# Attention and a gated feed-forward on one core: the engines' instructions in another order, found by a longer search

## The chip, the cores and the metric

The kernel runs on one core of a Trainium2 chip. The metric is the device time of one execution in microseconds, as the median of several runs.

## The reference

```python
q_d, k_d, v_d = mean over groups of 4 positions of q, k, v          # 576 -> 144
out_up = repeat(softmax(q_d k_d^T / 8) v_d, 4)
out_local = softmax(where(|i - j| < 4, q k^T / 8, -1e9)) v           # a band of 7
x = (out_up + out_local) as (batch * position, head * 64)            # 4608 x 512
out = ((x @ w1) * (x @ w2) @ w3) @ w_out
```

There are 8 batches of 8 heads, 576 positions and 64 dimensions; w1 and w2 are 512 x 1024, w3 is 1024 x 1024, w_out 1024 x 512. Activations are float32; the weights are given in 64 bits.

## The kernel before

**The fold.** Since nothing stands between w3 and w_out, their product is made once (`fold`, line 362 on): 64 products of 128 x 128 x 512, `accw`, each two matmul records. The 64-bit weights are loaded raw by SP (`words`, line 335) into a ring of six buffers `raw` and are turned to float32 by two passes on ScalarE (lines 342 and 350, the latter sometimes on VectorE, 354) and a join on VectorE (357). The gate weights w1 and w2 (`gate_weights`) come the same way, and are split into a high and a low part (436, 438).

**Attention.** For batches 0 to 2 it is done on TensorE: `pooled_sums` loads q and k in four phases (`q4` by line 635, `k4` by line 654), VectorE adds them up into `qks` (617) and reorders q into `qn` (641); `group_unit` makes the banded scores `se_ps` (723), `quad` the pooled scores `s_ps` (538), their maxima (543), exponentials (553), scaling (567 on ScalarE, 570 on GpSimd for later batches) and transposes `t_ps` (581), which ScalarE copies to `pt` (588, 590); `te_ps` and `pte` (693, 700) are the same of the banded scores. `group_values` and `pooled` multiply with v (`oe_ps` 772, `o_ps` 499). The pooled v is added up by GpSimd's accumulating DMAs (461). For batches 3 to 7 the banded part is done by VectorE and ScalarE (`unit`, line 857 on): products `pr` (884), their sums, a softmax, products `pv` with v, which are added up in `xl`, three of the six additions by an accumulating DMA that GpSimd issues (959).

**The feed-forward.** The 4608 tokens are nine chunks of 512. For each chunk and each f of 8, `moe` makes `pab` (two gates, 24 matmuls of 512 columns: three per product, with high and low parts), copies one on ScalarE (`a`, 1038), multiplies on VectorE (1040), splits into `gh` (ScalarE, 1044) and `gl` (VectorE, 1049), and multiplies with the folded weight into `acc` (`down`, 96 matmuls per f and four chunk rows of 128).

**What sets the order.** Every step is a task with an engine, a cost, what it needs and the buffers (`Ring`) it takes. The order on each engine is written out in `ORDER`, a table of task numbers by engine. `Plan.order` walks the five lists with the tasks' costs and merges them into one order of recording; it does not change the order within an engine. Semaphores then make each instruction wait for what it needs, and each engine takes its own list strictly in order.

```python
for e, l in mine.items():
    left[e] = [l[k] for w in ORDER[e].split() for a, _, b in [w.partition("-")] for k in range(int(a), int(b or a) + 1)][::-1]

def mm_us(n):
    return n * 0.418e-3 + 0.0135
```

Of the kernel before, what the change touches and what calls it, by code (L numbers as in the profile page):

```python
# [100 lines left out]
    ),  # L101
    DVE=(
# [164 lines left out]
def mm_us(n):  # L267
    return n * 0.418e-3 + 0.0135
# [973 lines left out]
```

## Time and profile before

| | |
|---|---|
| median of 3 runs | 778.26 us (775.34 to 779.37) |
| the profiled execution | 777.15 us, its span 775.0 us |
| TensorE busy | 748.4 us (97%), weight loads 574.7 us (74%) |
| VectorE busy | 575.0 us (74%) |
| ScalarE busy | 495.6 us (64%) |
| GpSimd busy | 136.0 us (18%) |
| HBM | 111 GB/s over the span |

The span runs from the first to the last instruction. The program has a first stage to about 104 us, in which the fold and the attention of the first tokens share TensorE while the queues load the weights; a middle in which the chunks' matmuls run while VectorE and ScalarE make the next tokens; and a last 120 us in which TensorE works alone. Busy times of TensorE overlap from one matmul to the next, and a matmul at half clock counts as busy.

### The profile page before, as it was taken

To read this page: it belongs to the slowest core of one execution; us is meant where nothing else is said; L and a number is where in the kernel's file an instruction comes from. 1 tells how busy PE (TensorE), PEld (TensorE's weight loads), DVE (VectorE), ACT (ScalarE), POOL (GpSimd) and SP (SyncE) were. 2 spreads that over 40 slices of the span, in tenths; PEclk is the share of its full clock that TensorE was granted. 3 is DMA by queue.
4 is the path that set the end of the run, shared out by engine and by line. 5 is a ranking of instruction groups with operands and counts; after the bars stand their busy time and mean duration, and the time that the engine had idled before them with its cause. 6 is when DMAs were issued, how large, how long until landed. Compare 5 with 4: busy or idle time off the path is not lost.

```text
span 775.0 us, 14532 instructions
## 1 busy us (share of the span) xinstructions
PE 748.4 (97%) x5140; PEld 574.7 (74%) x5140; DVE 575.0 (74%) x1041; ACT 495.6 (64%) x1910; POOL 136.0 (18%) x171
## 2 busy tenths in 40 slices
PE   2999999998999999999999999999999999999996
PEld 1454578776788887777777878787888778888885
DVE  4757877676557989899999999999898977422111
ACT  3976886458556777787877778687587647312111
POOL 1302001200220012511242224112330210100000
PEclk9999989999999999999999999999999999999999
DMA  9979734343552277758765876775654442211001
GB/s 295 299 225 293 251 106 134 62 117 84 143 107 111 66 179 184 127 133 207 184 118 138 213 151 152 193 166 143 151 115 122 126 93 55 41 22 35 20 1 54
DMA packets 53020, 104.94 MB, mean 135 GB/s; under 512 B 6204, under 2 KB 23612, under 8 KB 52948
## 3 DMA queue, kind: packets, MB, share of 16 engines
q1 hardware_dynamic: 39180, 70.13, 27.9%
q0 software_dynamic: 13632, 33.63, 25.6%
q8 instruction: 40, 0.66, 0.3%
q14 instruction: 32, 0.26, 0.1%
q10 hardware_dynamic: 136, 0.26, 0.1%
HBM read 76.87 MB, written 9.44 MB: 111 GB/s over the span
## 4 chain that ended last, share of the span: by engine, by line
PE 72%; DVE 11%; DMA 9%; ACT 3%; issue 3%; POOL 1%; SPq 1%; DVEq 0%; POOLq 0%
PE pab L310 14%; PE pab L312 13%; PE pab L311 13%; PE acc L310 7%; PE acc L312 6%; PE acc L311 6%; PE accw L392 4%; DMA vl<-in_v_dram 3%; PE o_ps L499 2%; DVE pr L884 2%; DMA xl<-pv 2%; PE oe_ps L772 1%; DVE pv L951 1%; DMA vs<-in_v_dram 1%; DVE gl L1049 1%
## 5 line engine op out<-in xcount | busy, mean ns | idle before, releaser
L310 PE MATMUL acc<-wphl,gh 128*128 128x512 f32 x288 | 115.5, 401 | 0.0
L312 PE MATMUL acc<-wphl,gl 128*128 128x512 f32 x288 | 113.1, 393 | 0.5 <-DVE gl L1049 0.5
L311 PE MATMUL acc<-wphl,gh 128*128 128x512 f32 x288 | 112.5, 391 | 0.0
L1040 DVE TENSOR_TENSOR a<-pab,a 128x512 f32<-128x512 f32 x72 | 49.4, 686 | 84.2 <-PE pab L312 72.2
L943 ACT ACTIVATE pv<-kv,s_t 128x64 f32<-128x64 f32 x360 | 96.2, 338 | 21.9 <-DVE s_t L920 15.6
L894 ACT ACTIVATE junk<-pr 128x64 f32<-128x64 f32 x360 | 92.1, 256 | 12.3 <-DVE pr L884 3.7
L884 DVE TENSOR_TENSOR pr<-q_t,kv 128x768 f32<-128x768 f32 x105 | 97.9, 955 | 1.7 <-DMA q_t<-in_q_dram 1.3
L1044 ACT CAST gh<-a 128x512 fp32r<-128x512 f32 x72 | 44.4, 617 | 75.9 <-PE acc L311 39.4
L959 POOL DMA_DIRECT2D xl<-pv x45 | 40.6, 901 | 260.4 <-DVE xl L961 190.0
L1038 ACT COPY a<-pab 128x512 f32<-128x512 f32 x72 | 41.9, 582 | 66.0 <-PE pab L312 50.6
L1049 DVE TENSOR_TENSOR gl<-a,gh 128x512 fp32r<-128x512 f32 x72 | 52.3, 726 | 28.4 <-ACT gh L1044 27.7
L897 DVE TENSOR_REDUCE s_t<-pr 128x12 f32<-128x768 f32 x75 | 70.1, 944 | 0.1
L894 ACT ACTIVATION_READ_ACCUMULATOR junk<-pr 128x1 f32 x360 | 67.5, 188 | 0.0
L461 POOL DMA_DIRECT2D vs<-in_v_dram x48 | 48.8, 1166 | 101.9 <-DMA vl<-in_v_dram 51.8
L392 PE MATMUL accw<-wo,wx 128*128 128x512 f32 x128 | 62.2, 625 | 2.2 <-DVE wx L357 2.2
L310 PEld LDWEIGHTS acc<-wphl,gh 128*128 128x128 f32 x288 | 54.1, 188 | 13.6 <-issue 2.5
L312 PEld LDWEIGHTS acc<-wphl,gl 128*128 128x128 f32 x288 | 54.1, 188 | 13.4 <-DVE gl L1049 1.4
L311 PEld LDWEIGHTS acc<-wphl,gh 128*128 128x128 f32 x288 | 54.2, 188 | 10.9
L310 PE MATMUL pab<-xh,wb 128*128 128x512 f32 x144 | 57.4, 399 | 0.6 <-DVE a L1040 0.6
L310 PE MATMUL pab<-xh,w1a 128*128 128x512 f32 x144 | 58.0, 402 | 0.0
L951 DVE TENSOR_TENSOR pv<-kv,s_t 128x768 f32<-128x768 f32 x60 | 57.7, 967 | 0.2
L310 PE MATMUL pab<-xh,wo 128*128 128x512 f32 x144 | 57.2, 397 | 0.7 <-ACT a L1038 0.7
(123 smaller groups left out, 1654.6 us busy)
## 6 DMA issues: line engine op xcount, KB each, us to landing
xl<-pv POOLq DMA_DIRECT2D x45, 384.0 KB, 4.3
raw<-in_w_dram SPq DMA_DIRECT2D x32, 512.0 KB
qks<-in_qk_dram POOLq DMA_DIRECT2D x15, 576.0 KB, 7.4
kv<-in_kw_dram SPq DMA_DIRECT2D x15, 576.0 KB
kv<-in_vw_dram SPq DMA_DIRECT2D x15, 576.0 KB
out_dram<-o_sb SPq DMA_DIRECT2D x24, 256.0 KB
q_t<-in_q_dram SPq DMA_DIRECT2D x15, 384.0 KB
raw<-in_wout_dram SPq DMA_DIRECT2D x8, 512.0 KB
```

What stands on the lines that cost most here:

```text
L310: nc.tensor.matmul(out_ps, lhsT=lh, rhs=rh, start=first, stop=False)
L311: nc.tensor.matmul(out_ps, lhsT=lh, rhs=rl, start=False, stop=False)
L312: nc.tensor.matmul(out_ps, lhsT=ll, rhs=rh, start=False, stop=last)
L392: nc.tensor.matmul(accs[m], lhsT=T["x"][:, at:at + 128], rhs=whole(j), start=j == 0, stop=j == NF - 1)
L461: dma = (lambda **kw: nc.gpsimd.dma_start(accum_op=ALU.add, **kw)) if add else nc.sync.dma_start
L884: (nc.gpsimd if o in share["qk_pool"] else nc.vector).tensor_tensor(out=T[o], in0=T["q"], in1=T["k"][:, o * D:o * D + nq].rearrange("p (t ...
L894: nc.scalar.activation(out=junk, in_=T[o][:, t], func=AF.Copy, accum_out=T["s"][:, t, o:o + 1])
L897: reds.append(add("DVE", dve_us(nq), lambda o=o: nc.vector.tensor_reduce(out=T["s"][:, :, o], in_=T[o], op=ALU.add, axis=AX.X), [tp], uses ...
L943: nc.scalar.mul(out=T["pv", o][:, tt], in_=T["v"][:, (tt + o) * D:(tt + o + 1) * D], mul=T["s"][:, tt, o:o + 1])
L951: nc.vector.tensor_tensor(out=T["pv", o], in0=T["v"][:, o * D:o * D + nq].rearrange("p (t d) -> p t d", d=D), in1=T["s"][:, :, o].unsqueez ...
L1040: tg = add("DVE", dve_us(size), lambda f=f: nc.vector.tensor_tensor(out=T["a", f], in0=T["p", 1, f][:, :size], in1=T["a", f], op=ALU.mult) ...
L1049: nc.vector.tensor_tensor(out=T["gl", f], in0=T["a", f], in1=T["gh", f].bitcast(F32), op=ALU.subtract)
```

## The change

The table `ORDER` is another one on all five engines, found by a search of five times the length, in which a matmul task costs a little more. The instructions, buffers and what waits for what by need are the same. Of the table one row tells a reader nothing; two of its lines and the whole of the rest of the diff are

```diff
     Pool=(
-        "1 0 4 2-3 5-6 8 7 11 9-10 14 13 12 17 15-16 18 20 19 21-23 25 24 26-27 30-31 29 28 34-35 32-33 38 37 36 40 39 43-45 52 46 56 "
...
+        "0-2 4-5 3 7 6 8-10 13 11-12 14 17 16 15 18 20 19 23 22 21 26 24-25 27 30-31 29 28 32 34 33 37-38 35-36 40 39 43-45 52 46 56 "
...
 def mm_us(n):
-    return n * 0.418e-3 + 0.0135
+    return n * 0.418e-3 + 0.018
```

Lines after the table stand one further down in the new kernel (L335 is now L336).

**The start, SP.** SP's first loads before; `q4` and `k4` are batch 0's, `raw` from in_wout and in_w3 are weights:

```order
L635 DMA q4_137<-in_qk4_dram 128x4x144
L335 DMA raw_139<-in_wout_dram 128x1024
L654 DMA k4_141<-in_qk4_dram 128x4x288
L635 DMA q4_143<-in_qk4_dram 128x4x144
L335 DMA raw_145<-in_w3_dram 128x4x256
L654 DMA k4_147<-in_qk4_dram 128x4x288
L335 DMA raw_149<-in_wout_dram 128x1024
```

and now:

```order
L336 DMA raw_137<-in_wout_dram 128x1024
L636 DMA q4_139<-in_qk4_dram 128x4x144
L655 DMA k4_141<-in_qk4_dram 128x4x288
L655 DMA k4_143<-in_qk4_dram 128x4x288
L636 DMA q4_145<-in_qk4_dram 128x4x144
L336 DMA raw_147<-in_w3_dram 128x4x256
L336 DMA raw_149<-in_wout_dram 128x1024
```

The second `k4` has moved ahead of the second `q4` and of the first block of w3. VectorE at the same place before, from the first sum over the second `k4` on:

```order
L617 TENSOR_TENSOR qks_161<-k4_147 128x288
L641 COPY qn_159<-q4_143 128x4x144
L617 TENSOR_TENSOR qks_161<-qks_161,q4_143 128x144 x2
L354 TENSOR_SCALAR raw_149<-raw_149 128x512
L543 TENSOR_REDUCE gmx_195<-s_ps_199 128x2
L543 TENSOR_REDUCE gmx_195<-s_ps_200 128x2
L617 TENSOR_TENSOR qks_161<-qks_161,k4_147 128x288
L357 SCALAR_TENSOR_TENSOR wx_168<-wx_168,raw_145 128x512
```

and now:

```order
L618 TENSOR_TENSOR qks_157<-k4_143 128x288
L642 COPY qn_159<-q4_145 128x4x144
L618 TENSOR_TENSOR qks_157<-qks_157,k4_143 128x288
L618 TENSOR_TENSOR qks_157<-q4_145 128x144
L618 TENSOR_TENSOR qks_157<-qks_157,q4_145 128x144 x2
L737 TENSOR_TENSOR se_192<-se_ps_173,band_88 128x216
L737 TENSOR_TENSOR se_192<-se_ps_174,band_88 128x216
L544 TENSOR_REDUCE gmx_196<-s_ps_200 128x2
L544 TENSOR_REDUCE gmx_196<-s_ps_201 128x2
```

Three sums of the second `q4` that stood ahead now follow its `qn`, a weight's low part (354) has gone from here, and the masks of the banded scores stand ahead of the maxima.

**The end of the first stage, ScalarE.** Before; `pexp` is the softmax of batch 1's second half, `raw` are gate weights:

```order
L350 ACTIVATE raw_1039<-raw_1039 128x512
L567 ACTIVATE pexp_77<-pexp_77,grs_1016 128x144
L567 ACTIVATE pexp_77<-pexp_77,grs_1016 128x128
L436 CAST w1a_79<-wx_1112 128x512
L567 ACTIVATE pexp_77<-pexp_77,grs_1016 128x128
L350 ACTIVATE raw_1074<-raw_1074 128x512
L567 ACTIVATE pexp_77<-pexp_77,grs_1016 128x144 x2
L700 COPY pte_1152<-te_ps_1138 72x3x2x64
L700 COPY pte_1152<-te_ps_1142 72x3x2x64
L342 ACTIVATE wx_1163<-raw_895 128x512
L342 ACTIVATE wx_1173<-raw_958 128x512
L588 COPY pt_997<-t_ps_1155 128x6x64
```

and now:

```order
L568 ACTIVATE pexp_77<-pexp_77,grs_1016 128x144
L568 ACTIVATE pexp_77<-pexp_77,grs_1016 128x128
L351 ACTIVATE raw_1039<-raw_1039 128x512
L437 CAST w1a_79<-wx_1116 128x512
L701 COPY pte_1144<-te_ps_1133 72x3x2x64
L701 COPY pte_1144<-te_ps_1137 72x3x2x64
L351 ACTIVATE raw_1083<-raw_1083 128x512
L343 ACTIVATE wx_1158<-raw_869 128x512
L343 ACTIVATE wx_1168<-raw_957 128x512
L589 COPY pt_997<-t_ps_1150 128x6x64
```

All scaling and the two copies to `pte` have moved ahead of the pass over the last gate weight of this stretch (`raw_1074` before, `raw_1083` now).

**Around 317 us, GpSimd.** Its issues before, from the last addition of unit 10 on (`xl`); `vs` and `vl` are the pooled v of batch 4, `qks` its q and k:

```order
L959 DMA xl_3511<-pv_3697 128x768
L461 DMA vs_3764<-in_v4_dram 56x512
L461 DMA vs_3764<-in_v4_dram 72x512
L477 DMA qks_3445<-in_qk4_dram 128x1152
L461 DMA vl_3765<-in_v4_dram 16x512
L461 DMA vs_3764<-in_v4_dram 72x512
L959 DMA xl_3820<-pv_3845 128x768
```

and now:

```order
L960 DMA xl_3501<-pv_3685 128x768
L478 DMA qks_3449<-in_qk4_dram 128x1152
L462 DMA vs_3767<-in_v4_dram 56x512
L462 DMA vs_3767<-in_v4_dram 72x512
L462 DMA vl_3768<-in_v4_dram 16x512
L960 DMA xl_3828<-pv_3887 128x768
L462 DMA vs_3767<-in_v4_dram 56x512
```

The first addition of unit 11 (`xl_3820`, now `xl_3828`) has moved ahead of every second addition to `vs` and `vl`.

## Rows read from the trace of the kernel before

**Rows 1.** The page, busy us (share of the span) and instructions.
```profile
PE 748.4 (97%) x5140; PEld 574.7 (74%) x5140; DVE 575.0 (74%) x1041; ACT 495.6 (64%) x1910; POOL 136.0 (18%) x171
```
**Rows 2.** TensorE's waits: us in total, times, the longest.
```profile
PE se_ps L723 <- DVE qn L641: 12.7, 2, 8.4
PE accw L392 <- DVE wx L357: 2.2, 2, 1.9
...
PE pab L310 <- DVE a L1040: 0.6, 1, 0.6
```
**Rows 3.** TensorE's timeline at the start: start, us, instruction, idle before.
```profile
13.18 0.86 PE L723 MATMUL se_ps<-k,qn 64*64 64x72 f32 x18 [4.28 <-DVE qn L641]
...
17.00 5.29 PE L392 MATMUL accw<-wo,wx 128*128 128x512 f32 x6 [1.88 <-DVE wx L357]
...
22.79 1.98 PE L392 MATMUL accw<-wo,wx 128*128 128x512 f32 x4
```
**Rows 4.** Stretches of 5 us: PE busy (instructions), clock, DMA share, GB/s.
```profile
100.00:105.00 5.00, 4.96 (x133) 0.55 0.60 194
105.00:110.00 5.00, 5.00 (x19) 0.77 0.40 127
```
**Rows 5.** TensorE's timeline at the end of the first stage.
```profile
97.81 0.55 PE L581 MATMUL t_ps<-ident,pexp 128*128 128x128 f32 x3 [0.71 <-ACT pt L588]
98.70 2.56 PE L772 MATMUL oe_ps<-pte,v_w 72*32 72x64 f32 x96 [0.35 <-ACT pte L700]
...
104.52 0.80 PE L310 MATMUL pab<-xh,w1a 128*128 128x512 f32 x1
```
**Rows 6.** VectorE's timeline at the start.
```profile
12.08 0.46 DVE L617 TENSOR_TENSOR qks<-k 128x288 f32<-128x288 f32 x1 [0.78 <-DMA k<-in_qk_dram]
12.45 0.67 DVE L641 COPY qn<-q 128x576 f32<-128x576 f32 x1
...
15.15 0.82 DVE L543 TENSOR_REDUCE gmx<-s_ps 128x2 f32<-128x288 f32 x2 [1.23 <-PE s_ps L538]
...
16.26 0.69 DVE L357 SCALAR_TENSOR_TENSOR wx<-wx,raw 128x512 int32<-128x512 int32 x1
```
**Rows 7.** DMA issues: what, how many, KB each.
```profile
raw<-in_w_dram SPq DMA_DIRECT2D x32, 512.0 KB
...
q<-in_qk_dram SPq DMA_DIRECT2D x12, 288.0 KB
```
**Rows 8.** Stretches: us; busy of PE, PEld, DVE, ACT, POOL; clock; DMA share; GB/s.
```profile
0.00:25.00 25.00, 10.45 (x78) 5.31 (x79) 14.61 (x50) 11.20 (x30) 5.57 (x21) 1.00 0.96 300
```
**Rows 9.** ScalarE's timeline at the end of the first stage.
```profile
94.23 0.68 ACT L350 ACTIVATE raw<-raw 128x512 int32<-128x512 uint16 x1 [0.77 <-DMA raw<-in_w_dram]
94.81 0.70 ACT L567 ACTIVATE pexp<-pexp,grs 128x144 f32<-128x144 f32 x2
...
96.15 1.24 ACT L342 ACTIVATE wx<-raw 128x512 f32<-128x512 f32 x2
97.29 0.46 ACT L588 COPY pt<-t_ps 128x384 f32<-128x384 f32 x1
```
**Rows 10.** GpSimd's timeline around 317 us.
```profile
317.11 0.83 POOL L461 DMA_DIRECT2D vs<-in_v_dram  x1 [3.38 <-DMA vs<-in_v_dram]
317.65 1.24 POOL L959 DMA_DIRECT2D xl<-pv  x1
```
**Rows 11.** VectorE's timeline after it.
```profile
323.90 0.96 DVE L961 TENSOR_TENSOR xl<-xl,pv 128x768 f32<-128x768 f32 x1 [2.03 <-DMA xl<-pv]
...
326.51 0.68 DVE L1040 TENSOR_TENSOR a<-pab,a 128x512 f32<-128x512 f32 x1
```
**Rows 12.** GpSimd's timeline around 444 us.
```profile
444.36 2.01 POOL L570 TENSOR_TENSOR pexp<-pexp,grs 128x432 f32<-128x432 f32 x2
```
**Rows 13.** VectorE's timeline: a gl at 312 us and the one at 444 us.
```profile
312.62 0.68 DVE L1049 TENSOR_TENSOR gl<-a,gh 128x512 fp32r<-128x512 f32 x1
...
444.39 2.54 DVE L1049 TENSOR_TENSOR gl<-a,gh 128x512 fp32r<-128x512 f32 x1 [0.18 <-issue]
```

175 rows, old and new, of tables (ACT, DVE, PE, Pool) are left out of this document.

## The prediction

> **What bounds the kernel now.** I first read the engines' shares, then the list of who waited for whom on TensorE, then the stretches, and last the timelines around the places where TensorE stood still. TensorE is busy for 97% of the span [rows 1], so by that share a new order of the same work can give back at most the other 26.6 us of 775.0. The list of TensorE's waits shows where half of that lies [rows 2]: 12.7 us at the first score matmuls, 2.2 us at the fold's matmuls (accw, the product of w3 and w_out), then single waits of well under 1 us. The busy share does hide something: six accw matmuls from 17.00 on take 5.29 us, four from 22.79 on take 1.98 us [rows 3]. That is 0.88 against 0.50 us each, half rate against nearly full, and both count as busy. The same comes back later: the granted clock is 0.55 of full in 100 to 105 us and 0.77 in 105 to 110 [rows 4], between the 1.2 and the 2.4 GHz level, although TensorE was never without work for more than 0.71 us just before [rows 5].
>
> So three places can pay: the start, the end of the first stage near 100 us, and single stalls behind VectorE later. Everything else of TensorE's program is the same count of matmuls in a row, and that costs the same in any order.
>
> **The change part by part.** No instruction is added or dropped. The number in the cost of a matmul task sets only in which order the five lists are merged; by itself it moves nothing within an engine, and I cost it at nothing.
>
> *The start.* TensorE's second half of the first scores waits until 13.18, and the fold's first accw until 17.00 [rows 3]. VectorE is what it waits for: it stands 0.78 us for a k4 load that it gets to at 12.08, only then makes the second qn at 12.45, waits 1.23 us for the scores at 15.15, and joins the first w3 block at 16.26 [rows 6]. Ahead of that k4 load SP now issues 288 + 512 KB less: a q4 and a w3 block stand behind it [rows 7]. The queues moved 300 GB/s in this stretch [rows 8], so 819,200 B are 2.7 us: the load lands near 9.3. The q4 that the second qn needs comes 288 KB later, 1.0 us, near 10.3. Then: qn done at 11.0 (0.6 us as now), five sums of 0.2 to 0.4 us to 12.0, the scores (1.2 us at half rate) to 13.2, two reductions to 13.95, the join to 14.7. The first accw then starts at about 14.8 in place of 17.0: 2.2 us earlier. The w3 block has as many bytes ahead of it as the k4 load has now, so it lands near 12.1, and ScalarE's two passes of 0.6 us end by 13.5, in time. The ends of this term are 0 (a load lands no earlier, since all queues are full) and 2.7 us (all of the bytes). I take 2.2, which is nearest to the row of VectorE's own sequence. What comes after must carry it: TensorE waited only 0.3 us more for weights after 17.00 (2.2 less the longest, 1.9) [rows 2], so the chain behind the start is TensorE's own work.
>
> *The end of the first stage.* ScalarE waits for a gate weight load until 94.23 and only then scales the last two softmax pieces (94.81); two more weight passes (96.15, 1.24 us) stand ahead of the copy of the transposed pieces at 97.29 [rows 9]. TensorE pays 0.71 us at 97.81 and 0.35 us at 98.70 [rows 5]. In the new order both the scaling and two te_ps copies stand ahead of that load's pass; the two weight passes still stand ahead of the pt copy. If the load lands at the same time, pt comes 1.3 us earlier (the 0.70 and the two copies are gone from the chain). TensorE can use 1.06 of it: I take 1.0. The ends are 0 (the load lands as much later) and 1.06.
>
> *The stall at 326 us.* GpSimd issues the add into xl at 317.65, behind a v add that had waited for its predecessor until 317.11 [rows 10]. VectorE then stands 2.03 us before 323.90, and the product a that TensorE's next task waits for begins at 326.51 [rows 11]; TensorE loses 0.6 us [rows 2]. Now that xl add stands two v adds earlier on GpSimd, ahead of the ones that wait for a predecessor: 0.6 us gained. The ends are 0 and 0.6.
>
> *Collisions of GpSimd and VectorE.* At 444.36 GpSimd runs its two multiplies of pexp, 2.01 us [rows 12]; the gl that VectorE began at 444.39 took 2.54 us, and another gl at 312.62 took 0.68 [rows 13]. The Trainium skill (SBUF — State Buffer, Who interferes with whom) says that a VectorE instruction with two SBUF inputs and a GpSimd instruction that reads SBUF shut each other out for a whole instruction; the trace agrees, with that 2.54. That rule speaks against an order found by adding costs, since the planner has no such lock. In the new order a gl stands within four VectorE instructions of the start of a GpSimd pair in three of ten cases, not as the first of them, and in three before: I put nothing in the sum, with ends of -1.9 and +1.9 us (one such gl more or fewer, 2.54 - 0.68).
>
> *The last tasks* end with the same block of rows, and only trade places before it: nothing.
>
> The sum is 2.2 + 1.0 + 0.6 = 3.8 us. The profiled execution took 777.15, so it would take 773.4. The median of the runs shown is 1.1 us above that execution; against the median, 778.26 - 3.8 = 774.5 us, and that is my forecast. A measurement of this kernel can tell about 0.5%, 3.9 us, from no change: the forecast stands right at that bound.
>
> **The rivals.** *The clock does not fall at the end of the first stage.* It gave 0.55 for 5 us and 0.77 for 5 us [rows 4], which is 2.25 + 1.15 = 3.4 us of full-rate work. If the waits at 97.81 and 98.70 vanish, the fall may too: 774.5 - 3.4 = 771.1. Against it: the same string of transposes and copies still stands there, and the waits may only shrink. The Trainium skill (TensorE: Matmul & The Clock Gate, What's actually happening) ties the fall to idleness of the engine; here it fell after waits of no more than 0.71 us [rows 5]. By that rule the time without the waits is that same 771.1.
>
> *The loads hold the first stage.* The DMA share is 0.96 in the first 25 us [rows 8] and the weights come through a ring of six buffers in SP's order. If the gate load that ScalarE meets at 94.23 lands no earlier, a start earlier by 2.2 us ends in a longer wait there, and only the 1.0 and a part of the 0.6 remain: about 777. For it: that row. Against it: TensorE's 0.3 us of waits for weights between.
>
> *Slower: the clock rises later.* TensorE's new list has the transposes of the first softmax right behind the first three products, where five products and a score task stood ahead of them before. They need ScalarE's scaling. If that is late, TensorE has a hole just where its first unbroken work lifts the clock (half rate from 17.00 until past 22, [rows 3]), and goes on at half rate. It decides if the pieces are ready later than three products at half rate, 3 x 1.76 = 5.3 us, after the first accw. Eight us more at half rate cost 4, and with the start's 2.2 lost and a hole of 2 the time is 778.26 - 1.6 + 4 + 2 = 782.7. By my reckoning the pieces are ready some 5 us after the first accw, so it is near.
>
> *More collisions.* Two stretched gl more in the stretch where VectorE is full eat 2 x 1.9 = 3.8 us if TensorE has to wait for all of it: 778, no change.
>
> **How the numbers follow.** The forecast 0.42 (0.22 faster, 0.20 within), no fall of the clock 0.20 (all faster), loads hold 0.20 (within, 0.02 of it slower), the later clock 0.11 (all slower), more collisions 0.07 (0.01 faster, 0.03 within, 0.03 slower). That makes faster 0.43, within 0.5% 0.41, slower 0.16. The range reaches from the case without the fall, less 1.5 us for a second stall saved, 769.6, to 780.5, which leaves out most of the slower case and little else.
>
> **What would show it.** In the profile after: the k4 load waited for near 9 to 10 us, the first accw near 15; no wait of 0.7 us at the last t_ps; the first gate matmul near 101 in place of 104.52 [rows 5]; no wait on an xl add near 320. The clock's stretch below full near 100 us, or its absence, tells the first rival; a gap of TensorE within 6 us of the first accw tells the slower one; a long wait of ScalarE or TensorE for raw between 85 and 100 us tells the loads. The forecast is wrong if the first gate matmul comes no earlier, or if TensorE's single waits after 200 us add up to more than now.

## The result, and the profile after

The new order took 771.31 us (median of 6 runs, 769.36 to 772.19), the old one 777.92 us beside it: a ratio of the means of 0.9909, 95% interval 0.9881 to 0.9937, or 7.1 us less (4.9 to 9.3). The forecast was 774.5. The profiled execution of the new order took 769.36 us, its span 767.6.

The engines' busy time on the page, to be read beside [rows 1]:

```profile
PE 743.8 (97%) x5140; PEld 573.1 (75%) x5140; DVE 574.6 (75%) x1041; ACT 495.0 (64%) x1910; POOL 135.1 (18%) x171
```

TensorE's five largest waits (us in total, times, the longest), which answer to [rows 2]:

```profile
PE se_ps L724 <- DVE qn L642: 11.3, 2, 8.2
PE accw L393 <- DVE wx L358: 1.7, 1, 1.7
PE o_ps L500 <- issue: 1.1, 2, 0.6
PE te_ps L694 <- DVE se L758: 0.5, 1, 0.5
PE pab L311 <- ACT oup L511: 0.4, 1, 0.4
```

The waits for "a" and for a "gl" are gone, and a new one stands there, at o_ps, for nothing that the profile can name.

**The start.** TensorE's timeline after (start, us, instruction, idle before), for [rows 3]:

```profile
11.77 0.86 PE L724 MATMUL se_ps<-k,qn 64*64 64x72 f32 x18 [3.10 <-DVE qn L642]
...
15.88 5.49 PE L393 MATMUL accw<-wo,wx 128*128 128x512 f32 x6 [1.71 <-DVE wx L358]
```

and VectorE's, for [rows 6]:

```profile
9.60 1.04 DVE L1168 COPY band<-xh 64x72 f32<-64x72 f32 x8
10.66 0.46 DVE L618 TENSOR_TENSOR qks<-k 128x288 f32<-128x288 f32 x1
11.04 0.67 DVE L642 COPY qn<-q 128x576 f32<-128x576 f32 x1
...
14.19 0.82 DVE L544 TENSOR_REDUCE gmx<-s_ps 128x2 f32<-128x288 f32 x2 [0.73 <-PE s_ps L539]
...
15.13 0.69 DVE L358 SCALAR_TENSOR_TENSOR wx<-wx,raw 128x512 int32<-128x512 int32 x1
```

VectorE no longer waits for the second k4; it comes to it at 10.66, behind its own work. The first accw comes at 15.88: 1.1 us earlier than before, where 2.2 were forecast.

**The end of the first stage.** TensorE, then ScalarE, for [rows 5, 9]:

```profile
96.39 1.86 PE L773 MATMUL oe_ps<-pte,v_w 72*32 72x64 f32 x96 [0.24 <-ACT pte L701]
...
100.44 0.50 PE L311 MATMUL pab<-xh,w1a 128*128 128x512 f32 x1 [0.42 <-ACT oup L511]
```

```profile
92.50 0.85 ACT L701 COPY pte<-te_ps 72x384 f32<-72x384 f32 x2
93.27 0.67 ACT L351 ACTIVATE raw<-raw 128x512 int32<-128x512 uint16 x1
...
94.99 0.46 ACT L589 COPY pt<-t_ps 128x384 f32<-128x384 f32 x1
```

ScalarE copies te_ps before it meets the raw load, which it now finds landed, and the copy to pt comes at 94.99 in place of 97.29; the wait of 0.71 us at the last t_ps is gone. And the clock (the last three columns are granted clock, DMA share, GB/s) stays at its upper level, where [rows 4] had 0.55 and 0.77:

```profile
100.00:105.00 5.00, 4.58 (x23) 3.80 (x21) 5.00 (x12) 5.00 (x12) 0.00 (x0) 1.00 0.31 118
105.00:110.00 5.00, 5.00 (x24) 4.14 (x23) 4.87 (x10) 5.00 (x11) 0.00 (x0) 1.00 0.00 0
```

The first gate matmul starts at 100.44 in place of 104.52. Of these 4.1 us, and of 1.2 more by the seventh gate matmul (107.25 before, 101.93 now), a large part is the clock (3.4 us by the prediction's count). By this pair of profiles the first rival has come about, and its 771.1 us are within 0.2 of the measured time. The runs below show that most of this reading does not hold.

**Later.** GpSimd issues the first xl addition of unit 11 at 309.53, and VectorE finds it landed ([rows 10, 11]: 317.65, and 2.03 us of wait). Where GpSimd's multiplies of pexp run, the gl that stood beside them [rows 12, 13] now begins just ahead of them and has its ordinary length; two small VectorE instructions behind it take 0.77 and 0.83 us; before, a pexp of this size took 0.21 at 443.84, and such an sm 0.17 at 447.11:

```profile
437.52 0.69 DVE L1050 TENSOR_TENSOR gl<-a,gh 128x512 fp32r<-128x512 f32 x1
...
438.27 0.77 DVE L573 TENSOR_TENSOR pexp<-pexp,grs 128x48 f32<-128x48 f32 x1
438.96 0.83 DVE L919 TENSOR_SCALAR sm<-sm 128x12 f32<-128x12 f32 x1
```

```profile
437.66 2.11 POOL L571 TENSOR_TENSOR pexp<-pexp,grs 128x432 f32<-128x432 f32 x2 [0.32 <-DVE s_t L912]
```

**The end** is longer. The last matmul starts at 768.23 before, 6.8 us ahead of the end of the span; now at 759.44, 8.1 us ahead of it. What the queues moved in 16 us, in 40 slices, before (from 760) and after (from 752):

```profile
GB/s 0 0 0 0 0 0 0 0 0 0 0 0 0 0 0 0 0 36 72 20 56 184 195 190 184 189 205 200 189 205 195 195 195 113 0 0 0 0 0 0
```

```profile
GB/s 0 0 0 0 0 0 0 0 0 0 0 0 0 0 0 31 72 26 56 189 189 159 82 123 179 179 118 92 113 179 174 189 200 174 92 5 0 0 0 0
```

The same 1.05 MB go out at an even 190 GB/s before, and with two sags now.

### The profile page after: what moved, and what is told of

It is laid out like the page before. It is cut to its first block, busy times and chain, and to the rows that moved or that the text cites. A ratio compares the mean times of both kernels' runs of the same rounds, so it can differ in the third digit from the quotient of the medians.

```text
span 767.6 us, 14527 instructions
## 1 busy us (share of the span) xinstructions
PE 743.8 (97%) x5140; PEld 573.1 (75%) x5140; DVE 574.6 (75%) x1041; ACT 495.0 (64%) x1910; POOL 135.1 (18%) x171
## 4 chain that ended last, share of the span: by engine, by line
PE 95%; ACT 2%; DVE 1%; DMA 1%; issue 0%; SPq 0%
PE pab L311 18%; PE pab L313 17%; PE pab L312 17%; PE acc L311 9%; PE acc L313 8%; PE acc L312 8%; PE accw L393 8%; PE o_ps L500 2%; PE s_ps L539 2%; PE oe_ps L773 2%; PE t_ps L582 2%; PE te_ps L694 1%; PE se_ps L724 1%; DMA raw<-in_wout_dram 1%; ACT se L755 1%; ACT wx L343 0%
## 5 line engine op out<-in xcount | busy, mean ns | idle before, releaser
L1050 DVE TENSOR_TENSOR gl<-a,gh 128x512 fp32r<-128x512 f32 x72 | 49.5, 687 | 37.4 <-ACT gh L1045 37.1
L952 DVE TENSOR_TENSOR pv<-kv,s_t 128x768 f32<-128x768 f32 x60 | 60.4, 1016 | 0.1
```

The lines of the kernel that those rows point to most:

```text
L952: nc.vector.tensor_tensor(out=T["pv", o], in0=T["v"][:, o * D:o * D + nq].rearrange("p (t d) -> p t d", d=D), in1=T["s"][:, :, o].unsqueez ...
L1050: nc.vector.tensor_tensor(out=T["gl", f], in0=T["a", f], in1=T["gh", f].bitcast(F32), op=ALU.subtract)
```

## The experiments

A "stretch" below is made so: the tasks of a stretch of the merged list keep their places, and stand in them in the new order; all others stand as in the old. The diffs of such kernels show only some rows of one engine, as a sample. A place where a stretch in one order meets the rest in the other is called a seam. A ratio is the kernel's time over that of the old order run beside it, with its 95% interval.

### Only the cost in the merge

```diff
-    return n * 0.418e-3 + 0.0135
+    return n * 0.418e-3 + 0.018
```

> The old order with only the dearer matmul in the merge's cost. Instructions on each engine are then the same rows in the same order. Expected by every theory: 0 us, within 0.3%. It is also a second profile of the old order: if the granted clock falls near 100 us because of where TensorE waits there, it falls again (0.5 to 0.8 in 100 to 110 us) and the first gate matmul starts near 104.5; if the fall was chance, it may be missing.

Ratio 1.0004 (0.9983 to 1.0026): nothing, as expected. But the second profile of the old order does not look like the first. TensorE and VectorE at 45 us, and the stretches:

```profile
46.65 1.12 PE L392 MATMUL accw<-wo,wx 128*128 128x512 f32 x2 [2.19 <-DVE wx L357]
```

```profile
44.92 0.42 DVE L481 COPY vl<-vl 16x512 f32<-16x512 f32 x1 [6.03 <-DMA vl<-in_v_dram]
```

```profile
45.00:50.00 5.00, 3.35 (x58) 1.76 (x62) 4.04 (x9) 3.09 (x10) 0.00 (x0) 0.82 0.52 148
50.00:55.00 5.00, 5.00 (x18) 2.05 (x10) 3.01 (x10) 4.20 (x14) 0.00 (x0) 0.50 0.46 146
...
100.00:105.00 5.00, 4.06 (x127) 2.93 (x124) 3.38 (x8) 5.00 (x12) 0.00 (x0) 1.00 0.60 200
105.00:110.00 5.00, 4.52 (x66) 3.46 (x63) 4.78 (x10) 5.00 (x12) 0.00 (x0) 1.00 0.46 138
```

VectorE stands 6 us at the copy of vl, which the third accumulating transfer has not finished; the join behind it comes late; TensorE stands 2.19 us, and the clock falls there, to the lower level (0.50). Near 100 us it doesn't fall. The same holds in four more profiles that have the old order up to 84 us (waits of 2.7 to 4.1 us at that accw; the clock at 0.50 to 0.71 in 50 to 55 us). In the profile that the prediction was made from, that wait was 0.3 us: it was the odd one of six.

```profile
45.37 1.13 PE L392 MATMUL accw<-wo,wx 128*128 128x512 f32 x2 [0.29 <-DVE wx L357]
```

The mean granted clock is on record for every run: 0.9955 over 30 runs of the old order (0.990 to 0.999), 0.9952 over the 6 of the new (0.993 to 0.997). Among the old ones 0.001 of clock goes with about 0.7 us. Over the whole study it was 0.9953 in 92 runs of the old order and 0.9962 in 25 of the four kernels that have the new first stage: 0.6 us by that. But the mean is taken over the whole span, and the clock also falls behind the last matmul, where no matmul pays for it. The stretches there, before and after:

```profile
769.00:775.00 6.00, 0.00 (x0) 0.00 (x0) 0.35 (x1) 0.00 (x0) 0.00 (x0) 0.82 0.39 144
760.00:767.50 7.50, 0.00 (x0) 0.00 (x0) 0.56 (x1) 0.00 (x0) 0.00 (x0) 0.64 0.38 120
```

That is 1.1 us of full-rate work before (6 us at 0.82) and 2.7 after, and in the profile after the clock is below full nowhere else. So the mean hides a part of the gain, and the clock has to be counted ahead of the last matmul. Around the first stage (40 to 112 us) it falls short by 3.4 us of full-rate work in four of the five profiles with the old first stage and by 1.7 in the fifth; by 1.7 in three of the four with the new one, and by nothing in the fourth. The means, 3.1 and 1.3, differ by 1.8 us. That is an estimate from nine profiles, and an upper one, since TensorE stood idle in a part of those stretches. So the clock is a smaller part of the 7 us, and it is not a fall near 100 us that the new order takes away.

### The start, the first stage, the rest

The start alone, here SP's rows:

```diff
-L635 DMA q_143<-in_qk_dram 128x4x144
+L654 DMA k_143<-in_qk_dram 128x4x288
+L635 DMA q_145<-in_qk_dram 128x4x144
 L335 DMA raw<-in_w_dram 128x4x256
-L654 DMA k_147<-in_qk_dram 128x4x288
```

> Only the tasks of about the first 25 us in the new order, on all engines; all later ones as before. Theory (the gain is of separate pieces: start 0.95, end of the first stage 4.4, later 3.4, tail -1.4): first accw at 15.9, TensorE 0.9 us ahead until about 90 us, clock falls near 100 us as before, so -0.9 us or less. Rival (the earlier start is what keeps the clock up): no fall near 100 us, -4 to -5 us. Rival (loads hold the first stage): ahead at 25 us, level with before at 94 us, 0 us.

Ratio 0.9979 (0.9956 to 1.0002), -1.6 us, with 0 just inside the interval. First accw at 15.62. The wait at the accw near 46 us was 3.6 us, as vl landed no earlier (copy at 45.13): a part of the start may be waited away there, but the old order alone has 0.3 to 4.1 us, so this is not shown. The clock fell at 45 us (0.66 in that stretch), not near 100 as the theory had it, and the first rival's -4 us did not come; the second rival, 0 us, is not excluded by time.

Everything to the second gate product, on all engines (shown are GpSimd's first additions, where two to vs and two to vl have left their old places):

```diff
 L461 DMA vs<-in_v_dram 56x512
-L461 DMA vl<-in_v_dram 16x512
-L461 DMA vs<-in_v_dram 72x512
-L461 DMA vl<-in_v_dram 16x512
-L461 DMA vs<-in_v_dram 72x512
 L461 DMA vl<-in_v_dram 16x512
```

> The new order for everything up to the second gate product of the first chunk (about 108 us), the old order after it. Theory of separate pieces: -5.3 us, granted clock at full in 100 to 110 us, first gate matmul near 100.5. Rival (what is gained early is waited away at the chunk boundary at 175 to 195 us, where VectorE and ScalarE set the pace): -2 us or less. Rival (most of the 7 us come from the single stalls after 150 us): -2 us or less, too, but with the whole gain lost nowhere in particular.

Ratio 0.9916 (0.9886 to 0.9946), -6.5 us: the first stage, as the theory said, and the rivals fall. Not for the reason expected of it alone: the clock did fall, at 45 to 55 us (0.95 and 0.71). Over this kernel's 7 runs the mean clock is 0.9974, the highest of the study, 0.0020 above the old order beside it; by 0.7 us for 0.001 that is up to 1.4 of the 6.5 us.

Everything after that product:

```diff
 L570 TENSOR_TENSOR pexp<-pexp,grs 128x3x128
-L959 DMA xl<-pv 128x768
+L959 DMA xl<-pv 128x768 x2
+L477 DMA qks<-in_qk_dram 128x1152
```

> The old order up to the second gate product of the first chunk (about 108 us), the new order after it. Theory of separate pieces: clock falls near 100 us as before, first gate matmul near 104.5, then 3.4 us gained between 150 and 620 us (stalls at 180 to 195, 326, 448 and 610 us), and the tail as it comes: -2 to -3.4 us. Rival (the late stalls vanish only because all comes earlier): 0 to -1 us.

Ratio 0.9962 (0.9936 to 0.9988), -3.0 us. The first gate matmul came at 108.03, as late as in the old order, and yet the rest was as quick as in the new one: the late gain does not hang on the early one. The two pieces add up to -9.5 us, more than the whole's -7.1, but no more than the three intervals allow.

The fourteen profiles of the study give a plain sum. First gate matmul: 104.5 to 109.2 in five with the old first stage (median 108.0), 100.4 to 103.1 in four with the new one (median 102.2). From there to the last matmul: 661.7 to 663.8 in eight with the old rest (mean 662.9), 659.0, 659.0, 659.0 and 660.4 with the new (659.3). From the last matmul to the end: 6.8 to 6.9 with the old tail, 8.0 and 8.1 with the new. That is -5.9 - 3.5 + 1.3 = -8.1 us, within the interval. The clock is in these numbers. Of the 5.9 it makes up to 1.8, by the estimate above. Near 198 us it falls too, which costs 1.7 us of full-rate work, in three of the eight profiles with the old rest and in one of the four with the new; and in the profile before, the fall near 100 us costs 1.4 us behind the first gate matmul. In the means that is 0.4 of the 3.5. The one of the four is the 660.4, shown here (e_best) ahead of a 659.0 (e_rest):

```profile
190.00:205.00 15.00, 14.09 (x175) 9.97 (x163) 5.72 (x15) 6.15 (x17) 0.00 (x0) 0.89 0.31 104
190.00:205.00 15.00, 13.61 (x231) 9.69 (x233) 4.79 (x14) 9.19 (x26) 0.79 (x1) 1.00 0.40 100
```

### The end of the first stage alone

ScalarE, whose pass over the last raw load goes behind the scaling and the copies:

```diff
-L350 ACTIVATE raw<-raw 128x512
-L567 ACTIVATE pexp<-pexp,grs 128x144 x2
-L700 COPY pte<-te_ps 72x3x2x64 x2
+L700 COPY pte<-te_ps 72x3x2x64 x2
+L350 ACTIVATE raw<-raw 128x512
```

> The old order with only the end of the first stage, from about 84 us to the second gate product of the first chunk, in the new one. Theory from four profiles of the old order and two of the new (the new order of this piece takes 1.4 us of waits away between the last weight product and the first gate products, and the clock has no part in it): -1.4 us, TensorE's waits at the last t_ps, oe_ps and o_ps of this stage together under 0.5 us in place of 1.0 to 1.4, mean granted clock over the runs as before's (0.995 to 0.996). Rival, the prediction's (those waits are what lowers the clock): -4 us and a mean clock higher by 0.004. Rival (the loads hold the first stage): 0 us, the waits only move to ScalarE's weight passes.

Ratio 0.9977 (0.9951 to 1.0002), -1.8 us, with 0 just inside the interval. TensorE's waits between 84 and 112 us:

```profile
PE pab L310 <- ACT oup L510: 0.5, 1, 0.5
PE oe_ps L772 <- ACT pte L700: 0.3, 1, 0.3
```

The wait at t_ps is gone; the mean clock is 0.9949 over 12 runs, 0.9948 over the 29 of the old order beside them, which have the same tail. The step was worth about what it was priced at, and the clock shows no part in it; the rival with -4 us falls.

### The boundary at 175 to 200 us, and the stretched gl

The stretch from 108 to 215 us (TensorE: a product of the folded weight has moved back):

```diff
-L310 MATMUL acc<-wphl,gh 128x512
-L311 MATMUL acc<-wphl,gh 128x512
-L312 MATMUL acc<-wphl,gl 128x512
 L310 MATMUL pab<-xh_666,w2a 128x512
```

> The old order with only the stretch from about 108 to 215 us in the new one, which holds the boundary from the first to the second chunk. Theory: TensorE's single waits between 175 and 200 us shrink from 3.3 to 4.0 us to about 2.6, so -1 us, not told from 0 by time. Rival (the waits shrink only because the whole first stage ended earlier): 0 us and the same gaps of 0.5 to 1.0 us between 180 and 198 us as before.

Ratio 0.9995 (0.9970 to 1.0021). TensorE's waits between 175 and 200 us, before and in this kernel:

```profile
PE te_ps L693 <- DVE se L757: 0.7, 1, 0.7
PE acc L312 <- DVE gl L1049: 0.5, 1, 0.5
PE o_ps L499 <- ACT pt L590: 0.4, 1, 0.4
PE te_ps L693 <- DVE pexp L572: 0.4, 1, 0.4
PE s_ps L538 <- ACT pt L588: 0.4, 1, 0.4
PE se_ps L723 <- DVE xl L803: 0.2, 1, 0.2
```

```profile
PE o_ps L499 <- issue: 0.5, 1, 0.5
PE te_ps L693 <- DVE se L757: 0.5, 1, 0.5
PE o_ps L499 <- ACT pt L590: 0.4, 1, 0.4
PE te_ps L693 <- ACT pexp L553: 0.4, 1, 0.4
```

2.6 against 1.8 us, and 1.8 too in the profile after, though this kernel's first gate matmul came at 109.24. So 0.8 us of waits are this stretch's own. Neither the time nor this profile shows them as a gain: from the first gate matmul to the last it took 663.2 us, within the old order's 661.7 to 663.8, as the clock fell near 199 us (0.83 in 195 to 205).

The stretch from 400 to 460 us (GpSimd):

```diff
-L461 DMA vs<-in_v_dram 72x512
-L959 DMA xl<-pv 128x768
-L461 DMA vs<-in_v_dram 72x512
+L461 DMA vs<-in_v_dram 72x512 x2
 L461 DMA vl<-in_v_dram 16x512
-L959 DMA xl<-pv 128x768
 L461 DMA vs<-in_v_dram 56x512
+L959 DMA xl<-pv 128x768 x2
```

> The old order with only the stretch from about 400 to 460 us in the new one. Theory (one gl of 2.54 us that runs beside GpSimd's two multiplies of pexp holds TensorE for 0.82 us near 449 us): no gl over 1.2 us before 460 us, the gap near 449 us gone, -0.8 us, not told from 0 by time; the later stretched gl near 610 us is still there. Rival (another VectorE instruction on the path is stretched in its place): a gap of the same size elsewhere between 400 and 470 us.

Slower: 1.0036 (1.0012 to 1.0059). The long gl near 444 us and TensorE's wait behind it are gone, and the later one (1.40 us, now at 617.7) is still there, as expected. But two other waits stand there, the first at the seam with the old order ahead of it, the second (1.3 us) at the seam behind it:

```profile
422.94 0.50 PE L310 MATMUL pab<-xh,w2a 128*128 128x512 f32 x1 [2.50 <-DVE a L1040]
```

```profile
PE o_ps L499 <- ACT pt L590: 1.8, 2, 1.3
```

The rival's gaps, but not its mechanism: at the first, VectorE had stood 3.99 us for an xl addition; the second was not followed back. What stands for the theory is that the gl of 2.5 to 2.8 us is in all nine profiles with the old order there, with 0.7 or 0.8 us of TensorE's wait for "a" behind it, and in none of the five with the new.

### The last rows

```diff
-        "692 713 693 716 694 714 718 695-696 720 722 697-698 717 699-700 723-724 721 728 725 729 727 732 726 731 730"
+        "692 713 693 716 694 714 718 695-696 720 722 697-698 717 699-700 723-724 721 728 725 729 732 727 731 726 730"
```

> The new order with the last four rows of the result ended in the old sequence (one pair of the last products of f = 6 and 7 changes places). Theory (in the new order the last two rows end 0.68 us apart in place of 1.36, so that the last store waits behind the one before it): from the start of the last matmul to the end of the span 6.8 us in place of 8.1, so -1.2 us against the new order, ratio to before about 0.989. Rival (the longer end is the stores' own chance): 6.8 to 8.1 us, no change.

Ratio 0.9888 (0.9860 to 0.9917), 770.39 us: the lowest ratio of the study, though the interval of the new order as it is (0.9881 to 0.9937) overlaps it. From the last matmul (761.30) to the end (768.1) 6.8 us, as the theory said. The copies of the last two rows begin at 760.37 and 761.73 here, at 759.19 and 759.87 in the profile after; so the 1.3 us come with two rows that end 0.68 us apart. That the last store waits behind the one before it is not shown.

### The transfers into vl

```diff
-        "1 0 4 2-3 5-6 8 7 11 9-10 14 13 12 17 15-16 18 20 19 21-23 25 24 26-27 30-31 29 28 34-35 32-33 38 37 36 40 39 43-45 52 46 56 "
+        "2 1 0 5 4 3 8 6-7 11 9-10 14 13 12 17 15-16 18 20 19 21-23 25 24 26-27 30-31 29 28 34-35 32-33 38 37 36 40 39 43-45 52 46 56 "
```

> The old order on every engine but GpSimd, whose first nine accumulating transfers (three each into the two parts of vs and into vl of batch 0) change places: each round of three begins with vl. Theory (in the old order the third addition to vl lands at 43.6 to 47.8 us, VectorE stands 4 to 8 us at the copy of vl, and TensorE 2.2 to 4.1 us at the weight product whose join is queued behind that copy): the copy comes before 41 us, TensorE's wait there is under 0.5 us, the half-clock stretch after it is gone from most runs, -3 to -5 us. Rival (the transfers' queues are full, so one chain is quicker only at another's cost): the additions to vs land later by as much, TensorE waits at its first o_ps instead, 0 to -1 us. Rival (the time lost near 45 us is waited for near 95 us anyway): waits near 45 us gone, but the first gate matmul at the same 106 us, 0 us.

The copy came at 39.45 and the wait at the accw was gone, but the time stayed: 0.9993 (0.9966 to 1.0020). The theory's -3 to -5 us are excluded. The first rival's wait for vs did not come; the second rival, that the same time is waited for later, fits: the first gate matmul came at 104.89, within the old order's 104.5 to 109.2. TensorE stands a little later, for nothing that the profile names:

```profile
48.29 0.47 PE L499 MATMUL o_ps<-pt,vl 16*32 16x144 f32 x12 [1.20 <-issue]
```

and the clock falls behind that (0.68 in 50 to 55 us). A late vl is one wait of this place, not the only one. The same edit on the kernel with the mended tail (GpSimd's row of the new table):

```diff
-        "0-2 4-5 3 7 6 8-10 13 11-12 14 17 16 15 18 20 19 23 22 21 26 24-25 27 30-31 29 28 32 34 33 37-38 35-36 40 39 43-45 52 46 56 "
+        "2 0-1 5 4 3 8 7 6 9-10 13 11-12 14 17 16 15 18 20 19 23 22 21 26 24-25 27 30-31 29 28 32 34 33 37-38 35-36 40 39 43-45 52 46 56 "
```

> The new order with the old sequence of the last rows, as before, and with GpSimd's first nine transfers in rounds that begin with vl. Theory: TensorE's 0.6 to 1.9 us of wait at the first products with vl (o_ps near 49 us) vanish, so -1 us against the kernel with the old tail alone, near 769.5 and ratio 0.987 to 0.988. Rival (the vs additions become the late ones): the wait moves to the o_ps with vs, 0 to +1 us.

0.9889 (0.9855 to 0.9923), the same as without it. vl was copied at 40.02, and the wait at o_ps was 2.21 us, the longest of all: it does not come from a late vl, and the theory falls.

### Two pieces that don't fit alone

25 to 60 us (TensorE, the end of batch 0's first half):

```diff
-L392 MATMUL accw<-wo,wx 128x512 x3
-L581 MATMUL t_ps<-ident,pexp 128x128 x6
-L693 MATMUL te_ps<-ident,se 72x128 x6
 L392 MATMUL accw<-wo,wx 128x512 x2
+L581 MATMUL t_ps<-ident,pexp 128x128 x3
+L392 MATMUL accw<-wo,wx 128x512
 L772 MATMUL oe_ps<-pte,v_w 32x64 x48
-L581 MATMUL t_ps<-ident,pexp 128x128 x3
```

> The old order with only the stretch from about 25 to 60 us in the new one (here vl's additions keep their old start). Theory (what the new order gains here is that no weight product of TensorE is queued behind the copy of vl, and less waiting on vl): TensorE's wait at accw gone, 0.6 to 2 us at o_ps in its place, -1.5 to -2.5 us. Rival (only the earlier start of vl's first addition counts): as much waiting as before in another place, 0 us.

1.0034 (1.0014 to 1.0055), slower, where -1.5 to -2.5 us were expected. The waits near 45 us went as the theory said, without a fall of the clock, but 3.06 us of wait for xl stand at 90.61, behind the seam, and the clock falls there. So the time says nothing for the stretch itself. And everything to 84 us (SP: the first loads of batch 1's v go behind gate weights):

```diff
+L335 DMA raw<-in_w_dram 128x1024
+L676 DMA v_w<-in_v_dram 18x512 x4
 L462 DMA vs<-in_v_dram 72x512
 L463 DMA vs<-in_v_dram 56x512
 L464 DMA vl<-in_v_dram 16x512
-L676 DMA v_w<-in_v_dram 18x512 x4
-L335 DMA raw<-in_w_dram 128x4x256
```

> The new order for everything up to about 84 us, the old order after it. Known: the start alone gave -1.6 us, the end of the first stage alone -1.5, everything to 108 us -6.5, and the stretch from 25 to 60 us alone came out slower because TensorE waited 3 us at its seam with the old order. Theory (the new order gains some 3 us between 25 and 84 us, once the start and this stretch belong together): -4 to -5 us, TensorE's wait at accw near 46 us gone. Rival (nothing is gained there; the rest of the 6.5 us needs the end of the stage with it): -1.5 to -2 us. Where a wait of 1 us or more stands at the seam near 84 to 95 us, the time says nothing for either.

1.0089 (1.0063 to 1.0114), slower, and by the condition set there without a verdict. TensorE and VectorE at the seam:

```profile
95.08 0.99 PE L723 MATMUL se_ps<-k,qn 64*64 64x72 f32 x22 [6.98 <-DVE xl L803]
```

```profile
92.99 0.42 DVE L481 COPY vl<-vl 16x512 f32<-16x512 f32 x1 [8.29 <-DMA vl<-in_v_dram]
```

SP's new list brings batch 1's v later, VectorE's old list copies its vl early, and all that is queued behind that copy waits. In the new order the copy stands behind the weights too (96.73, before 83.15). So it looks as if two engines' lists carry this step together.

## Why the prediction came out as it did

The side was right and 771.31 lies within the range; the size was not: 3.8 us forecast, 7.1 measured.

- **The start, -2.2.** Mis-sized. The first accw came at 15.5 to 15.9 in the six profiles with the new start, at 16.5 to 17.7 in the eight with the old (means 15.75 and 17.2): 1.4 us. The step that failed is the reckoning along VectorE's sequence, "qn done at 11.0": the load was there, but eight copies of band (1.04 us) still stood ahead of the second k4 sum, so qn began only at 11.04 and the sum behind it at 11.54; the sums took 0.3 us and the scores 0.2 us more than reckoned. By time the start alone gave 1.6 us, with 0 just inside the interval.
- **The end of the first stage, -1.0.** Right in mechanism; -1.8 by time, with 0 just inside the interval.
- **The rest of the first stage, not in the sum.** 5.9 us came out of the first stage and only 3.2 were forecast. What lies between 25 and 84 us was costed at nothing, since one profile showed one wait of 0.3 us there. Five others had 2.2 to 4.1. The start's 1.4 and the end's 1.8 leave 2.7 us. By the profiles up to 1.8 of that are the clock, which in four of the five old ones falls behind that wait. How the 2.7 divide between the clock, vl's addition and the weights that now pass batch 1's v stays open: the pieces could not be cut out without a seam.
- **The stall at 326 us, -0.6.** The xl addition came early as forecast. But the old order's stall was 0.6 us in this one profile, 0.2 to 0.4 in five others and nothing in four: a mean of 0.2.
- **Collisions, 0 (-1.9 to +1.9).** Within its ends: the stretched gl at 444 us, with 0.7 us of TensorE's wait, is in no profile of the new order. The rows after agree with the rule of the Trainium skill that the prediction cites (SBUF — State Buffer, Who interferes with whom): the pexp beside GpSimd's pair, which has two SBUF inputs, takes 0.77 us in place of 0.21. VectorE is still held there, but in small instructions that TensorE does not wait for. What failed was the count of near pairs in the lists: it does not tell which instruction meets the pair.
- **"Everything else of TensorE's program costs the same in any order."** That step failed most: from the first gate matmul to the end of the matmuls the new order is 3.5 us quicker. By TensorE's waits 0.8 is the boundary, 0.7 the gl, 0.2 the xl addition and 0.2 a wait at t_ps near 611 us; some 0.4 is the clock (the plain sum above). The rest, 1.2, was not taken apart.
- **The tail, 0.** Wrong by 1.3 us to the other side: trading places of two products decides how close the last stores follow each other.
- **The merge's cost, 0.** Right.
- **The rival with the clock, 771.1.** Its time fits, and so does the pair of profiles, but that is luck: by the estimates above the clock makes at most some 2 us of the 7, not 3.4 on top of the forecast's 3.8, and the end of the stage alone did not move it. What the rival took for a mark of the old order was the place of the fall in one execution.
- **The slower rival.** TensorE had no hole behind the first accw; t_ps followed at 21.16.
- **The rival with the loads.** ScalarE waits for no raw load between 85 and 100 us in the profile after (its last such wait is 0.64 us, at 84.90), and the first stage ended earlier.
- **More collisions.** After 200 us no wait of TensorE is left on the list after, where before there were 1.5 us in three.

## What to carry to other kernels

While the queues are full, the same program waits by another amount in every execution (0.3 to 4.1 us at one accw), and its clock falls in another place: take a second profile (a no-op edit will do) before pricing a wait or a fall of the clock, and use the mean clock of all runs only less what lies behind the last matmul. Follow an in-order engine's copy that waits for a chain of accumulating transfers: all that is queued behind it waits too, although here taking this one wait away gained nothing by itself. An order found for all engines together can have steps that two engines carry between them; this one could be split where the pieces meet at a narrow place (the first gate product) and hardly elsewhere; and the last rows deserve a look of their own, by when their stores start.

## What the runs showed that was not expected

TensorE stands in the middle of the products with vl, after the 14th of 32 (after the 20th in the old order with vl's transfers moved), for nothing that the profile names. TensorE after the change, and the queues of the profile after between 46 and 47 us:

```profile
48.23 0.47 PE L500 MATMUL o_ps<-pt,vl 16*32 16x144 f32 x14
49.29 0.65 PE L500 MATMUL o_ps<-pt,vl 16*32 16x144 f32 x18 [0.59 <-issue]
```

```profile
q8 instruction: 1, 0.02, 7.1%
```

One packet of 16 KB of the instruction queue lands at 47.88 there, and TensorE goes on 1.4 us later; in five other profiles with such a wait (1.2 to 2.2 us) it goes on 1.3 to 1.5 us after that packet. In the six profiles with the old order up to 84 us TensorE comes to its place, after the 20th, 1.3 to 5.9 us after the packet, and does not stand. So it looks as if the engine had run out of instructions while the data queues were full (the DMA share in 40 to 45 us was 1.03). That was read from times alone and not tried.
